# Maxima over partitions by TensorE transposes, and fewer loads for keys and values

## The chip, the cores and the metric

The kernel runs on one core of a Trainium2 chip. A core has five engines with a queue of instructions each: PE (TensorE, matmuls; the profile shows its weight loads apart, as PEld), DVE (VectorE), ACT (ScalarE), POOL (GpSimd) and SP (SyncE, which here only issues DMAs). An engine takes its queue in order, and a semaphore holds an instruction back until what it needs is there. The metric is the time of one execution on the device in microseconds, lower is better.

## The reference

Three layers follow each other, all in float32.

```python
# memory attention: B=8 batches, H=8 heads, S=576 positions, d=64, M=32 memory slots
a = exp(phi - max(phi, axis=2));  a = a / (sum(a, axis=2) + 1e-09)      # over the 576 positions
k_m = einsum('bhsm,bhsd->bhmd', a, k);  v_m = einsum('bhsm,bhsd->bhmd', a, v)
scores = q @ k_m.T / 8
attn = exp(scores - max(scores, -1));  attn = attn / (sum(attn, -1) + 1e-09)
x = (attn @ v_m) with heads side by side                                # 4608 x 512
# first feed-forward layer: w_in 512 x 2048, w_out 2048 x 512
h = x @ w_in;  x = (h - tanh(h)) @ w_out
# second: w1, w2, w3 512 x 768, w_out 768 x 512
y = maximum(maximum(x @ w1, x @ w2), x @ w3) @ w_out                    # 4608 x 512, the output
```

The softmax weights `a` need, for each batch, head and memory slot, the largest of 576 values of phi. The kernel puts positions on the 128 partitions, so this maximum runs along the free axis and then over partitions.

## The kernel before, in words

**Precision.** The two feed-forward layers and the product with attn split each operand into a high and a low float32r part and add three matmuls (`mm3`, lines 93 to 96). Weights are converted from the two halves of a 64-bit word to float32 (`conv`, lines 99 to 124: a load, ACT, five DVE instructions, POOL).

**The attention of one batch.** `load_phi` brings phi as 128 partitions x 8 heads x 5 chunks x 32 slots (the fifth chunk has 64 positions, the rest is filled with -3e38). `phi_gen` (lines 176 to 192) takes the maximum over the chunks (`mx`, DVE), then over the partitions by POOL's `partition_all_reduce` (`mxa`), subtracts it (DVE), and takes exp (ACT). `kv_mm` (lines 198 to 228) multiplies the weights with keys and values: for each parity `e` of the head, chunk `c` and head pair `r`, one float32 matmul of 32 columns of weights with 129 columns, of which 64 are keys, 64 values and one a constant one, so that the sum of the weights falls out beside. It accumulates in the PSUM tile `ps_kv`. Then come the division (`rc`, `n`, DVE), a transpose by matmuls with `ident` (`ps_t`) and the copies `kT`, `vT` (ACT). `q_gen` (lines 239 to 283) transposes the queries (DVE), makes scores (`sc`), the softmax over 32 slots, and the split weights `at`. `vw_gen` multiplies `vT` with a quarter of W_in (`wi`, from `wi_conv`) to `vw`, so that the first layer is one product of `at` and `vw`.

**Loads.** All of these DMAs are issued by SP. Keys and values of a head pair fill one of four tiles by six DMAs (`load_kv`, lines 151 to 162; 256-byte pieces in the large ones), 24 a batch. Queries are sixteen DMAs a batch in pieces of 128 bytes. phi is one tile and is loaded again for the next batch once `kv_mm` has read it, and so are the key and value tiles.

**The feed-forward stream.** A step is one 128-wide slice `fc` of the hidden layer for 288 positions: six matmuls into `ps_h` (`emit_h`), tanh on ACT, the difference on DVE (`th`), the high part on ACT and the low part on POOL (`gh`, line 404), then twelve matmuls into `ps_x` (`emit_x`). h runs three steps ahead of x, gh two. The first half of the hidden layer (phase 0) runs batch after batch beside the attention of the batches to come, the second half (phase 1) after it beside the conversion of the last layer's weights; then the last layer follows alone.

**What sets the order.** The code hands the attention's generators out in slots between the stream's matmuls, each with the step from which it may run (`kv_gen` of a batch 20 steps before its first). A prelude drains the first batch's `phi_gen`, `kv_mm`, half of `q_gen` and the first quarter of W_in (lines 480 to 486). A scheduler then rearranges the instructions of each engine by its own model of times, which moves urgent ones ahead. The PSUM pool `ps_m` has two buffers for all of `ps_kv`, `ps_t`, `sc` and `ps_w`.

Of the kernel before, what the change touches and what calls it, by code (L numbers as in the profile page):

```python
# [1 line left out]

# [4 lines left out]

F32 = mybir.dt.float32
# [3 lines left out]
ALU = mybir.AluOpType  # L12
AX = mybir.AxisListType
# [9 lines left out]
def kernel(  # L23
# [23 lines left out]
    V, S, G, T, DMA = nc.vector, nc.scalar, nc.gpsimd, nc.tensor, nc.sync  # L47
    B, H, NS, D = q.shape
    M = phi.shape[3]
    P = 128  # L50
    HP = H // 2
    C = 5
    KV = 2 * D + 2
    NKV = 4
    TJ = NS // 32
    JH = TJ // 2
    NH = NS // 2
# [9 lines left out]
    def pool(name, space=None, stack=ctx, **kw):  # L67
        if space is not None:
            kw["space"] = space
        if space is not DRAM:  # L70
            kw["reuse_waits"] = "tile"
        return stack.enter_context(tc.tile_pool(name=name, bufs=1, **kw))

    dram = pool("dram", DRAM)
    const = pool("const")
    ident = const.tile([P, P], F32, name="ident")

    main, wo_s = ExitStack(), ExitStack()
    wo_p = pool("wo", stack=wo_s, side="right")
# [5 lines left out]
    ap = pool("attn", stack=attn)  # L85
    ps_x = pool("ps_x", PSUM, main)
    ps_h = pool("ps_h", PSUM, main)
    ps_m = pool("ps_m", PSUM, main)
# [47 lines left out]
    phi_t, kv_t, q_t = {}, {}, {}  # L136

    def load_phi(b):
        if b < B and b not in phi_t:
            t = ap.tile([P, H, C, M], F32, tag="phi", bufs=1, name="phi")  # L140
            DMA.dma_start(out=t[:, :, :4], in_=phi[b, :, :4 * P].rearrange("h (p c) m -> p h c m", p=P))
            DMA.dma_start(out=t[:64, :, 4], in_=phi[b, :, 4 * P:].rearrange("h p m -> p h m"))
            G.memset(t[64:, :, 4], -3e38)
            phi_t[b] = t


    kv_s = [ap.tile([P, 2, C, KV], F32, name=f"kv{i}") for i in range(NKV)]
    kv_order = [(b, r) for b in range(B) for r in range(HP)]
    kv_next = [0]

    def load_kv():
        if kv_next[0] < len(kv_order):
            b, r = kv_order[kv_next[0]]
            t = kv_s[kv_next[0] % NKV]
            kv_next[0] += 1
            for i, x in enumerate((k, v)):
                src = x[b, 2 * r:2 * r + 2]
                o = slice(i * D, i * D + D)
                for h in range(2):
                    DMA.dma_start(out=t[:, h, :4, o], in_=src[h, :4 * P].rearrange("(p c) d -> p c d", p=P))  # L160
                DMA.dma_start(out=t[:64, :, 4, o], in_=src[:, 4 * P:].rearrange("h p d -> p h d"))
            kv_t[b, r] = t


    def load_q(b, g):
        if b < B and (b, g) not in q_t:
            t = ap.tile([P, 2, TJ, 32], F32, tag="q", bufs=2, name="qt")
            src = q[b, 4 * g:4 * g + 4].rearrange("(r e) (p j) (t d) -> e t r p j d", e=2, p=32, t=2)
            for e in range(2):
                for h in range(2):  # L170
                    for r in range(2):
                        DMA.dma_start(out=t[64 * e + 32 * h:64 * e + 32 * h + 32, r], in_=src[e, h, r])
            q_t[b, g] = t
# [3 lines left out]
    def phi_gen(b):  # L177
        load_phi(b)
        ph = phi_t.pop(b)
        yield  # L180
        mx = ap.tile([P, H, M], F32, tag="mx", bufs=1, name="mx")
        V.tensor_reduce(mx, ph.rearrange("p h c m -> p h m c"), axis=AX.X, op=ALU.max)
        yield
        mxa = ap.tile([P, H, M], F32, tag="mxa", bufs=1, name="mxa")
        G.partition_all_reduce(mxa.rearrange("p h m -> p (h m)"), mx.rearrange("p h m -> p (h m)"), P, bass_isa.ReduceOp.max)
        yield
        V.tensor_tensor(out=ph, in0=ph, in1=mxa[:, :, None, :].to_broadcast([P, H, C, M]), op=ALU.subtract)
        yield
        S.activation(ph, ph, AF.Exp)
        yield  # L190
        ph_t[b] = ph
        yield
# [5 lines left out]
    def kv_mm(b):  # L198
        ph = ph_t.pop(b)
        ps = ps_m.tile([P, 2, 256], F32, tag="m", bufs=2, name="ps_kv")  # L200
        ts = [kv_t.pop((b, r)) for r in range(HP)]
        for e in range(2):
            for c in range(C):
                pk = P if c < 4 else 64
                for r in range(HP):
                    T.matmul(ps[32 * r:32 * r + 32, e, :2 * D + 1], ph[:pk, 2 * r + e, c], ts[r][:pk, e, c, :2 * D + 1], start=c == 0, stop=c == C - 1)
                if c % 2:
                    yield
            yield
        load_phi(b + 1)  # L210
        for r in range(HP):
            load_kv()
        rc = ap.tile([P, 2], F32, tag="rc", bufs=2, name="rc")
        V.tensor_scalar(rc, ps[:, :, 2 * D], 1e-9, None, ALU.add)
        V.reciprocal(rc, rc)
        n = ap.tile([P, 2, 2, D], F32, tag="kvn", bufs=2, name="n")
        V.tensor_tensor(out=n.rearrange("p i e d -> p e i d"), in0=ps[:, :, :2 * D].rearrange("p e (i d) -> p e i d", i=2),
                        in1=rc[:, :, None, None].to_broadcast([P, 2, 2, D]), op=ALU.mult)
        yield
        pt = ps_m.tile([P, 2, P], F32, tag="m", bufs=2, name="ps_t")  # L220
        for i in range(2):
            for e in range(2):
                T.matmul(pt[64 * e:64 * e + 64, i], n[:, i, e], ident, start=True, stop=True)
        kT[b] = ap.tile([P, HP, M], F32, tag="kT", bufs=2, name="kT")
        for i, t in enumerate((kT[b], vT[b])):
            S.copy(t.rearrange("p r m -> p (r m)"), pt[:, i])
        yield

    def kv_gen(b):
        yield from phi_gen(b)  # L230
        yield from kv_mm(b)
# [134 lines left out]
    steps, start = [], {}  # L366
# [95 lines left out]

    V.memset(ident, 0.0)
    G.affine_select(ident, ident, pattern=[[-1, P]], compare_op=ALU.not_equal, fill=1.0, base=0, channel_multiplier=1)
    for t in kv_s:
        G.memset(t[:, :, :, 2 * D:], 1.0)
    def drain(*gens):
        gens = list(gens)
        while gens:
            for g in list(gens):  # L470
                try:
                    next(g)
                except StopIteration:
                    gens.remove(g)
# [3 lines left out]
            yield from g  # L478

    load_phi(0)  # L480
    for _ in range(NKV):
        load_kv()
    drain(phi_gen(0))
    drain(chain(kv_mm(0), q_gen(0, (0,))), wi_conv(0))
    drain(vw_gen(0, 0, 0))
    drain(wo_conv(0, wo_p), q_gen(0, (1,)))
# [171 lines left out]
```

## Time and profile before

| | us |
|---|---|
| median of 3 runs (1539.48 to 1541.59) | 1541.33 |
| the profiled execution | 1544.93 |
| its span | 1543.0 |
| PE busy | 1386.9 |
| DVE busy | 652.6 |
| POOL busy | 487.0 |
| ACT busy | 442.5 |

The profile shows one execution. Busy times are those of an engine at work on an instruction; waits and issues of DMAs are not counted. A row's name is "out <- in" by the program's tiles, with the line of the kernel. In the timeline and the groups, the brackets or the last column give the idle time of the engine before a row and what ended it; "issue" means that the profile shows nothing it waited for. [...]

### The profile page before, as it was taken

The page shows a single profiled execution, that of the slowest core. Times are in us where ns is not written, and L with a number is a line of the kernel's source. Part 1 is how long each engine was busy: PE and PEld are TensorE (multiplying, and loading weights), DVE is VectorE, ACT ScalarE, POOL GpSimd, SP SyncE. Part 2 cuts the span into 40 slices and gives each one's busy share as a digit, 9 for nine tenths or more (in the row PEclk, how much of TensorE's full clock was granted, in tenths as well). Part 3 has the DMA queues.
Part 4 walks back from the last instruction along what each step waited for, and adds up shares of the span by engine and source line. Part 5 has one row for each costly group of instructions (what it writes and reads, how often), then busy time and mean ns, then how long its engine had stood idle before and what let it go on. Part 6 is the DMA issues. An engine that isn't in the chain of part 4 may idle for free.

```text
span 1543.0 us, 22485 instructions
## 1 busy us (share of the span) xinstructions
PE 1386.9 (90%) x8672; PEld 1159.2 (75%) x8672; DVE 652.6 (42%) x1209; ACT 442.5 (29%) x975; POOL 487.0 (32%) x519
## 2 busy tenths in 40 slices
PE   1468596977979989999999999999999999999998
PEld 1147385866868767888799998888888888888887
DVE  3567685444454896878732322212121121221111
ACT  1224342333434444444433332111111111111110
POOL 1245452342333666656633333111111111111110
PEclk8579898988989999999999999999999999999999
DMA  7665555544441536787522117201011010100001
GB/s 172 153 135 163 145 160 126 139 120 103 105 117 47 176 101 200 252 263 239 196 97 85 48 62 255 92 14 42 21 41 48 14 42 14 48 14 21 14 14 41
DMA packets 250858, 159.81 MB, mean 104 GB/s; under 512 B 164224, under 2 KB 233856, under 8 KB 248960
## 3 DMA queue, kind: packets, MB, share of 16 engines
q1 hardware_dynamic: 249024, 145.80, 33.9%
q0 software_dynamic: 1728, 12.58, 2.2%
q8 instruction: 68, 1.11, 0.3%
q14 instruction: 38, 0.31, 0.1%
HBM read 105.64 MB, written 52.69 MB: 103 GB/s over the span
## 4 chain that ended last, share of the span: by engine, by line
PE 50%; DVE 4%; DMA 4%; POOL 1%; issue 1%; SPq 1%; ACT 1%; POOLq 0%; ACTq 0%; DVEq 0%
PE ps_w L96 10%; PE ps_w L95 10%; PE ps_w L94 10%; PE ps_o L95 3%; PE ps_o L94 3%; PE ps_o L96 3%; PE ps_x L95 3%; PE ps_x L96 3%; PE ps_x L94 2%; DMA wb_d<-cs 2%; PE ps_h L94 1%; PE ps_h L96 1%; PE ps_h L95 1%; POOL cs L123 1%; SPq L321 1%
## 5 line engine op out<-in xcount | busy, mean ns | idle before, releaser
L95 PE MATMUL ps_x<-gh,wo 128*128 128x288 f32 x1024 | 303.5, 305 | 51.0 <-POOL gh L404 50.9
L404 POOL TENSOR_TENSOR gh<-th,gh 128x288 fp32r<-128x288 f32 x256 | 220.0, 861 | 336.6 <-ACT gh L403 270.8
L96 PE MATMUL ps_x<-gh,wo 128*128 128x288 f32 x1024 | 297.9, 301 | 1.6 <-POOL wo L123 1.5
L94 PE MATMUL ps_x<-gh,wo 128*128 128x288 f32 x1024 | 263.7, 305 | 16.7 <-ACT wo L121 10.0
L96 PE MATMUL ps_w<-xh,wb 128*128 128x512 f32 x648 | 254.9, 393 | 0.0
L95 PE MATMUL ps_w<-xh,wb 128*128 128x512 f32 x648 | 254.4, 393 | 0.0
L94 PE MATMUL ps_w<-xh,wb 128*128 128x512 f32 x648 | 253.8, 392 | 0.0
L95 PEld LDWEIGHTS ps_x<-gh,wo 128*128 128x128 f32 x1024 | 197.9, 193 | 74.4 <-POOL gh L404 60.8
L598 POOL TENSOR_TENSOR mh<-m,mh 128x512 fp32r<-128x512 f32 x54 | 71.1, 1319 | 489.1 <-ACT mh L597 489.1
L401 DVE TENSOR_TENSOR th<-ps_h,th 128x288 f32<-128x288 f32 x256 | 115.5, 452 | 230.2 <-ACT th L400 230.1
L94 PEld LDWEIGHTS ps_x<-gh,wo 128*128 128x128 f32 x1024 | 181.7, 194 | 39.7 <-issue 11.9
L96 PEld LDWEIGHTS ps_x<-gh,wo 128*128 128x128 f32 x1024 | 197.6, 194 | 3.5 <-POOL wo L123 2.1
L94 PE MATMUL ps_h<-at,vw 128*128 128x288 f32 x512 | 158.7, 311 | 14.7 <-DVE th L401 13.1
L594 DVE TENSOR_TENSOR m<-ps_w,m 128x512 f32<-128x512 f32 x54 | 37.4, 692 | 305.5 <-PE ps_w L96 305.5
L403 ACT CAST gh<-th 128x288 fp32r<-128x288 f32 x256 | 110.5, 432 | 166.6 <-DVE th L401 146.3
L400 ACT ACTIVATE th<-ps_h 128x288 f32<-128x288 f32 x256 | 104.3, 409 | 186.1 <-PE ps_h L96 153.7
L95 PE MATMUL ps_h<-at,vw 128*128 128x288 f32 x512 | 153.7, 300 | 0.3 <-POOL at L279 0.3
L96 PE MATMUL ps_h<-at,vw 128*128 128x288 f32 x512 | 153.9, 301 | 0.0
L95 PEld LDWEIGHTS ps_w<-xh,wb 128*128 128x128 f32 x648 | 121.7, 188 | 27.9
L94 PEld LDWEIGHTS ps_w<-xh,wb 128*128 128x128 f32 x648 | 121.7, 188 | 27.5
L96 PEld LDWEIGHTS ps_w<-xh,wb 128*128 128x128 f32 x648 | 121.7, 188 | 27.2
L94 PEld LDWEIGHTS ps_h<-at,vw 128*128 128x128 f32 x512 | 98.7, 193 | 41.0 <-DVE th L401 23.4
(74 smaller groups left out, 1743.2 us busy)
## 6 DMA issues: line engine op xcount, KB each, us to landing
xd<-xo SPq DMA_DIRECT2D x36, 576.0 KB, 3.6
raw<-in_moe_w_out_dram SPq DMA_DIRECT2D x22, 512.0 KB, 3.5
qt<-in_q_dram SPq DMA_DIRECT2D x128, 72.0 KB, 3.1
at_d<-at SPq DMA_DIRECT2D x16, 576.0 KB, 3.6
at<-at_d SPq DMA_DIRECT2D x8, 1152.0 KB, 6.0
raw<-in_moe_w_dram SPq DMA_DIRECT2D x24, 384.0 KB, 3.6
wb_d<-cs SPq DMA_DIRECT2D x72, 128.0 KB, 2.9
xo<-xd SPq DMA_DIRECT2D x16, 576.0 KB, 4.3
```

Source lines behind the costliest of these rows:

```text
L94: T.matmul(o, w[0], x[0], start=start, stop=False)
L95: T.matmul(o, w[0], x[1], start=False, stop=False)
L96: T.matmul(o, w[1], x[0], start=False, stop=stop)
L123: G.tensor_sub(lo, f(a), f(hi))
L321: DMA.dma_start(out=wb_d[3 * g + i][:, w, kc], in_=f(t[:, :, i * P:(i + 1) * P]))
L400: S.activation(th, ps, AF.Tanh)
L401: V.tensor_sub(th, ps, th)
L403: S.copy(gh[:, 0], th)
L404: G.tensor_sub(gh[:, 1], th, f(gh[:, 0]))
L594: V.tensor_max(m, pss[1], m)
L598: G.tensor_sub(mh[:, 1], m, f(mh[:, 0]))
```

## The change

Four things are changed. The maximum over partitions goes through PE: `mx` (128 partitions x 256 columns, head and slot) is transposed in two halves into the PSUM tile `ps_mx`, DVE reduces each row to one number (`mt`, 128 x 2), multiplies it onto the diagonal of `ident` (`dg`), and a matmul of `ones` with `dg` gives every partition all 256 maxima, which the subtraction reads from PSUM. The pool's two PSUM buffers now serve `ps_mx` too. Second, keys and values of a batch lie in one tile, filled by four DMAs (1 KB pieces in the two large ones), issued once `kv_mm` of the batch before has run. Third, the sum of the weights has matmuls of its own, of one column against `ones`, ahead of the matmuls of 128 columns. Fourth, the first batch's queries are loaded before the first pieces of W_in, not after them.

```diff
-    kv_s = [ap.tile([P, 2, C, KV], F32, name=f"kv{i}") for i in range(NKV)]
...
-    def load_kv():
...
-                for h in range(2):
-                    DMA.dma_start(out=t[:, h, :4, o], in_=src[h, :4 * P].rearrange("(p c) d -> p c d", p=P))
-                DMA.dma_start(out=t[:64, :, 4, o], in_=src[:, 4 * P:].rearrange("h p d -> p h d"))
-            kv_t[b, r] = t
+    def load_kv(b):
+        if b < B:
+            t = kv_t[b] = ap.tile([P, 2, H, C, D], F32, tag="kv", bufs=1, name="kv")
+            for i, x in enumerate((k, v)):
+                DMA.dma_start(out=t[:, i, :, :4].rearrange("p h c d -> p h (c d)"), in_=x[b, :, :4 * P].rearrange("h (p c) d -> p h (c d)", p=P))
+                DMA.dma_start(out=t[:64, i, :, 4], in_=x[b, :, 4 * P:].rearrange("h p d -> p h d"))
@@ phi_gen
-        mxa = ap.tile([P, H, M], F32, tag="mxa", bufs=1, name="mxa")
-        G.partition_all_reduce(mxa.rearrange("p h m -> p (h m)"), mx.rearrange("p h m -> p (h m)"), P, bass_isa.ReduceOp.max)
-        yield
-        V.tensor_tensor(out=ph, in0=ph, in1=mxa[:, :, None, :].to_broadcast([P, H, C, M]), op=ALU.subtract)
+        pm = ps_m.tile([P, 2, 2, P], F32, tag="m", bufs=2, name="ps_mx")
+        for i in range(2):
+            T.transpose(pm[:, 0, i], mx[:, 4 * i:4 * i + 4].rearrange("p h m -> p (h m)"), ident)
+        mt = ap.tile([P, 2], F32, tag="mt", bufs=1, name="mt")
+        V.tensor_reduce(mt, pm[:, 0], axis=AX.X, op=ALU.max)
+        yield
+        dg = ap.tile([P, 2, P], F32, tag="dg", bufs=1, name="dg")
+        V.tensor_tensor(out=dg, in0=ident[:, None, :].to_broadcast([P, 2, P]), in1=mt[:, :, None].to_broadcast([P, 2, P]), op=ALU.mult)
+        T.matmul(pm[:, 1].rearrange("p i j -> p (i j)"), ones, dg.rearrange("p i j -> p (i j)"), start=True, stop=True)
+        yield
+        V.tensor_tensor(out=ph, in0=ph, in1=pm[:, 1].rearrange("p i (h m) -> p (i h) m", m=M)[:, :, None, :].to_broadcast([P, H, C, M]), op=ALU.subtract)
@@ kv_mm
-                    T.matmul(ps[32 * r:32 * r + 32, e, :2 * D + 1], ph[:pk, 2 * r + e, c], ts[r][:pk, e, c, :2 * D + 1], start=c == 0, stop=c == C - 1)
+                    T.matmul(ps[32 * r:32 * r + 32, e, 2 * D:2 * D + 1], ph[:pk, 2 * r + e, c], ones[:pk, :1], start=c == 0, stop=c == C - 1)
+            for c in range(C):
+                pk = P if c < 4 else 64
+                for r in range(HP):
+                    T.matmul(ps[32 * r:32 * r + 32, e, :2 * D], ph[:pk, 2 * r + e, c], t[:pk, :, 2 * r + e, c], start=c == 0, stop=c == C - 1)
...
-        for r in range(HP):
-            load_kv()
+        load_kv(b + 1)
...
-    for t in kv_s:
-        G.memset(t[:, :, :, 2 * D:], 1.0)
+    G.memset(ones, 1.0)
...
-    for _ in range(NKV):
-        load_kv()
+    load_kv(0)
+    load_q(0, 0)
+    load_q(0, 1)
     drain(phi_gen(0))
```

The scheduler puts the instructions of every engine in another order with it. Three places matter below. SP's queue at the start of the program, before (kv_88 to kv_91 are the four key and value tiles, raw a piece of a weight matrix, qt the queries; of the first batch's 24 loads two rows stand, and the x14 come after the 24 of the second batch, of which the last two rows stand):

```order
L141 DMA phi<-in_phi_dram 128x8x128
L142 DMA phi<-in_phi_dram 64x8x32
L160 DMA kv_88<-in_k_dram 128x4x64 x2
L161 DMA kv_88<-in_k_dram 64x2x64
...
L101 DMA raw<-in_moe_w_in_dram 128x1024 x2
L172 DMA qt<-in_q_dram 32x18x32 x2
...
L160 DMA kv_91<-in_v_dram 128x4x64 x2
L161 DMA kv_91<-in_v_dram 64x2x64
L172 DMA qt<-in_q_dram 32x18x32 x14
L101 DMA raw<-in_moe_w_in_dram 128x1024 x2
```

and now:

```order
L140 DMA phi<-in_phi_dram 128x8x128
L141 DMA phi<-in_phi_dram 64x8x32
L150 DMA kv<-in_k_dram 128x8x256
L151 DMA kv<-in_k_dram 64x8x64
L150 DMA kv<-in_v_dram 128x8x256
L151 DMA kv<-in_v_dram 64x8x64
L161 DMA qt<-in_q_dram 32x18x32 x16
L100 DMA raw<-in_moe_w_in_dram 128x1024 x2
L161 DMA qt<-in_q_dram 32x18x32 x2
...
L100 DMA raw<-in_moe_w_in_dram 128x1024
L161 DMA qt<-in_q_dram 32x18x32 x5
L100 DMA raw<-in_moe_w_in_dram 128x1024
```

The first sixteen query loads moved from behind both batches' keys and values to a place ahead of W_in; behind them, the second batch's keys and values still stand ahead of the last pieces of W_in.

[...]

```order
L404 TENSOR_TENSOR gh<-th,gh 128x288 x7
L143 MEMSET phi 64x8x32
L404 TENSOR_TENSOR gh<-th,gh 128x288
L185 ISA
L185 ISA mxa<-mx 128x256
L404 ISA
L404 TENSOR_TENSOR gh<-th,gh 128x288 x4
L273 TENSOR_TENSOR s<-s,st 128x288 x2
L404 TENSOR_TENSOR gh<-th,gh 128x288
L279 TENSOR_TENSOR at<-aT,at 128x288 x2
```

and now:

```order
L403 TENSOR_TENSOR gh<-th,gh 128x288 x8
L142 MEMSET phi 64x8x32
L403 TENSOR_TENSOR gh<-th,gh 128x288 x4
L272 TENSOR_TENSOR s<-s,st 128x288 x2
L278 TENSOR_TENSOR at<-aT,at 128x288
L403 TENSOR_TENSOR gh<-th,gh 128x288
L278 TENSOR_TENSOR at<-aT,at 128x288
```

The reduction and the ISA rows around it are gone, and gh follows gh.

PE's queue around a batch's `kv_mm` in phase 0, before (the first rows of the 40; ps_x and ps_h are the stream):

```order
L95 MATMUL ps_h<-at,vw 128x288
L96 MATMUL ps_h<-at,vw 128x288
L94 MATMUL ps_x_3052<-gh,wo_1182 128x288
L206 MATMUL ps_kv<-kv_88,phi 32x129
L206 MATMUL ps_kv<-kv_89,phi 32x129
L206 MATMUL ps_kv<-kv_90,phi 32x129
L206 MATMUL ps_kv<-kv_91,phi 32x129
L206 MATMUL ps_kv<-kv_88,phi 32x129
```

and now, in the same part of the program, with the transposes, the matmul by ones and `kv_mm` in three pieces:

```order
L175 MATMUL ps_mx<-ident,mx 128x128 x2
L93 MATMUL ps_x_2491<-gh,wo_1170 128x288
...
L95 MATMUL ps_h<-at,vw 128x288
L181 MATMUL ps_mx<-dg,ones 128x256
L93 MATMUL ps_h<-at,vw 128x288
...
L93 MATMUL ps_h<-at,vw 128x288
L202 MATMUL ps_kv<-ones,phi 32x1 x20
L206 MATMUL ps_kv<-kv,phi 32x128 x20
L202 MATMUL ps_kv<-ones,phi 32x1 x20
L206 MATMUL ps_kv<-kv,phi 32x128 x20
L93 MATMUL ps_x_2845<-gh,wo_559 128x288
```

The transposes and the matmul by ones stand between the stream's matmuls, 31 rows apart, and 44 rows ahead of `kv_mm`, which now has forty matmuls of one column beside forty of 128.

## Rows read from the trace of the kernel before

**Rows 1.** busy time by stage: length, engines (instructions), granted clock, DMA share, GB/s.

```profile
0.00:69.67 69.67, 15.91 (x121) 5.71 (x121) 26.45 (x50) 9.99 (x16) 11.66 (x21) 0.70 0.74 161
69.67:256.49 186.82, 135.01 (x1067) 106.02 (x1067) 131.61 (x248) 65.78 (x154) 83.78 (x86) 0.84 0.58 152
256.49:437.47 180.98, 152.81 (x1320) 130.54 (x1320) 83.88 (x183) 64.18 (x154) 61.39 (x79) 0.91 0.49 117
```

**Rows 2.** Waits of PE up to 560 us: total, times, longest.

```profile
PE ps_x L95 <- POOL gh L404: 50.0, 7, 10.5
...
PE ps_t L223 <- DVE n L217: 12.7, 3, 5.2
```

**Rows 3.** Timeline of POOL: start, length, instruction, [idle before <- what ended it].

```profile
371.82 1.08 POOL L185 PARTITION_ALL_REDUCE mxa<-mx  x1 [6.37 <-PE ps_h L96]
380.78 1.54 POOL L404 TENSOR_TENSOR gh<-th,gh 128x288 fp32r<-128x288 f32 x2 [7.88 <-issue]
```

**Rows 4.** Timeline of PE, same columns: first and last stall.

```profile
110.15 0.61 PE L94 MATMUL ps_x<-gh,wo 128*128 128x288 f32 x1 [9.38 <-ACT wo L121]
...
437.47 0.61 PE L95 MATMUL ps_x<-gh,wo 128*128 128x288 f32 x1 [9.00 <-POOL gh L404]
```

**Rows 5.** Busy time by stretch, as rows 1: after the stalls, and their sum.

```profile
110.15:119.50 9.35, 9.35 (x43) 6.96 (x44) 5.10 (x15) 3.90 (x9) 3.62 (x6) 0.50 0.17 26
192.26:198.00 5.74, 5.74 (x34) 4.55 (x35) 2.92 (x8) 2.39 (x7) 1.10 (x2) 0.50 0.37 95
...
sum 35.08, PE 35.07 PEld 27.61 DVE 17.72 ACT 11.52 POOL 13.22; mean PE 5.85 PEld 4.60 DVE 2.95 ACT 1.92 POOL 2.20
```

**Rows 6.** Timeline of PE and of its weight loads (PEld): kv_mm, ps_t.

```profile
293.98 0.30 PE L95 MATMUL ps_x<-gh,wo 128*128 128x288 f32 x1
294.12 0.29 PE L96 MATMUL ps_x<-gh,wo 128*128 128x288 f32 x1
294.34 2.82 PE L206 MATMUL ps_kv<-kv,phi 128*32 128x129 f32 x80
...
294.34 0.82 PEld L206 LDWEIGHTS ps_kv<-kv,phi 128*32 128x32 f32 x32 [0.16 <-issue]
295.36 0.15 PEld L206 LDWEIGHTS ps_kv<-kv,phi 64*32 64x32 f32 x8 [0.20 <-issue]
...
364.41 0.66 PE L223 MATMUL ps_t<-ident,n 128*64 128x128 f32 x8
```

**Rows 7.** The tile ps_kv: duration in ns, least/median/most.

```profile
L206 PE MATMUL ps_kv<-kv,phi x640: 270/273/424, 12.0 to 481.4; 128*32 128x129 f32 x128, 64*32 64x129 f32 x32
```

**Rows 8.** Groups by line, to 800 us: busy us, mean ns, idle before.

```profile
L182 DVE TENSOR_REDUCE mx<-phi 128x256 f32<-128x1280 f32 x8 | 19.4, 2424 | 12.5 <-DMA phi<-in_phi_dram 12.5
...
L187 DVE TENSOR_TENSOR phi<-phi,mxa 128x1280 f32<-128x1280 f32 x8 | 11.9, 1492 | 32.1 <-POOL mxa L185 32.1
...
L189 ACT ACTIVATE phi<-phi 128x1280 f32<-128x1280 f32 x8 | 10.2, 1269 | 42.9 <-DVE phi L187 37.4 <-DMA kv<-in_v_dram 5.5
...
L217 DVE TENSOR_TENSOR n<-ps_kv,rc 128x256 f32<-128x256 f32 x8 | 3.3, 418 | 0.1
```

**Rows 9.** Timeline of SP's queue (SPq), the first 70 us.

```profile
2.04 1.30 SPq L160 DMA_DIRECT2D kv<-in_k_dram  x2
...
17.35 0.63 SPq L161 DMA_DIRECT2D kv<-in_v_dram  x1
...
40.27 9.38 SPq L172 DMA_DIRECT2D qt<-in_q_dram  x14
49.77 1.41 SPq L101 DMA_DIRECT2D raw<-in_moe_w_in_dram  x2
```

**Rows 10.** Timeline of PE, the first 72 us.

```profile
19.08 4.95 PE L206 MATMUL ps_kv<-kv,phi 128*32 128x129 f32 x74 [3.53 <-DMA kv<-in_v_dram]
...
47.58 1.30 PE L257 MATMUL sc<-qT,kT 64*32 64x288 f32 x8 [17.33 <-DVE qT L248]
...
69.67 0.61 PE L94 MATMUL ps_h<-at,vw 128*128 128x288 f32 x1 [0.67 <-ACT vw L298]
```

More of the change, by code (lines that the diff above doesn't have):

```diff
@@ L4 @@
 import concourse.tile as tile
-from concourse import bass_isa, mybir
+from concourse import mybir
 from concourse._compat import with_exitstack
@@ L52 @@
     C = 5
-    KV = 2 * D + 2
-    NKV = 4
     TJ = NS // 32
@@ L76 @@
     ident = const.tile([P, P], F32, name="ident")
+    ones = const.tile([P, P], F32, name="ones")
     main, wo_s = ExitStack(), ExitStack()
@@ L144, in load_phi @@
             phi_t[b] = t
-    kv_s = [ap.tile([P, 2, C, KV], F32, name=f"kv{i}") for i in range(NKV)]
-    kv_order = [(b, r) for b in range(B) for r in range(HP)]
-    kv_next = [0]
-    def load_kv():
[L152 to L155, printed above, removed]
-            for i, x in enumerate((k, v)):
-                src = x[b, 2 * r:2 * r + 2]
-                o = slice(i * D, i * D + D)
-                for h in range(2):
-                    DMA.dma_start(out=t[:, h, :4, o], in_=src[h, :4 * P].rearrange("(p c) d -> p c d", p=P))
-                DMA.dma_start(out=t[:64, :, 4, o], in_=src[:, 4 * P:].rearrange("h p d -> p h d"))
-            kv_t[b, r] = t
+    def load_kv(b):
+        if b < B:
+            t = kv_t[b] = ap.tile([P, 2, H, C, D], F32, tag="kv", bufs=1, name="kv")
+            for i, x in enumerate((k, v)):
+                DMA.dma_start(out=t[:, i, :, :4].rearrange("p h c d -> p h (c d)"), in_=x[b, :, :4 * P].rearrange("h (p c) d -> p h (c d)", p=P))
+                DMA.dma_start(out=t[:64, i, :, 4], in_=x[b, :, 4 * P:].rearrange("h p d -> p h d"))
     def load_q(b, g):
@@ L200, in kv_mm @@
         ps = ps_m.tile([P, 2, 256], F32, tag="m", bufs=2, name="ps_kv")
-        ts = [kv_t.pop((b, r)) for r in range(HP)]
+        t = kv_t.pop(b)
         for e in range(2):
```

## The prediction

> **What bounds the kernel now.** I read the stage table first, then who TensorE waits for, then the timeline of the engine that it names. The stage table [rows 1] cuts the span at the first matmul that makes h (69.67 us), after the fourth batch's reduction on POOL (256.49) and after the last (437.47). Behind that no instruction is added or taken away. Up to 69.67 us PE is busy for 15.91 of 69.67 us: a prelude of loads and preparation. From there to 437.47 us PE is busy for 135.01 of 186.82 and 152.81 of 180.98 us, at a mean granted clock of 0.84 and 0.91. DVE is the next engine: 131.61 of 186.82 us in the middle, 83.88 of 180.98 after it.
>
> The waits [rows 2] put the largest share of PE's idle time on POOL's gh: 50.0 us in seven waits. The timeline of POOL around one of them [rows 3] shows why. The reduction over partitions is a row of 1.08 us, but POOL stands idle 6.37 us ahead of it and 7.88 us behind it, with nothing that it waits for: from 365.45 (371.82 less 6.37) to 380.78 us POOL makes no gh, and PE, two steps ahead at most, runs dry. It happens once a batch; the first two batches fall into the prelude, and six stalls are left, the first and the last of which stand in [rows 4]: 9.38 + 10.48 + 10.03 + 9.35 + 9.82 + 9.00 = 58.06 us. (The first is put down to ACT's wo cast, which itself waited for POOL.) [...]
>
> [...]
>
> **The change, part by part.**
>
> *POOL's reduction goes.* In the new order of POOL gh follows gh at that place, with no custom instruction, so no stretch of [rows 3] is left: -58.1 us and -17.5 us, if nothing else is late at those places.
>
> *PE gets new work, which goes straight onto the path.* The column of ones leaves the value tile, so kv_mm issues 40 more matmuls of one column a batch, 80 in the profile's records, which show each of these float32 matmuls twice. The old 80 take 2.82 us at full clock [rows 6], with weights loaded every 0.82/32 = 26 ns, and 0.20 us lost where the shape changes from 128 to 64 rows or back. One column can hardly go faster than its weight load: 80 x 26 ns = 2.05 us, and four more changes of shape are 0.8 us, 2.85 in all. Bounds: 1 us, if such a matmul hides in its neighbours; 5.4 us, if the twenty records of a column group follow each other at the 0.27 us that one of the old ones lasts [rows 7]. I take 2.85, since the weight loads are the same. The two transposes and the matmul by ones are six records; eight of the ps_t row take 0.66 us [rows 6], so 0.5 us and about 0.35 us to fill twice: 0.85. That is 3.7 us a batch, 1.5 to 6.2. Batch 0's share is in the prelude; seven are 25.9 us.
>
> *DVE gets two small instructions*, the maximum over 256 PSUM elements and the diagonal: each like the 0.418 us of n, a 256-element read of PSUM [rows 8]. The subtraction stays 1.49 us. 0.84 us a batch, beside PE in the last stage, and counted below in the middle one.
>
> *A chain PE - DVE - PE - DVE - ACT takes the place of POOL's.* PE now waits in its queue for the maxima (transposes) and for the diagonal (matmul by ones), and behind the waiting matmul stand the next h and x matmuls. In the new order some 30 matmul rows lie between the two, about 4 us of PE work at 0.13 to 0.14 us each, the distance of two in [rows 6], and 44 more, 5.9 us, from there to kv_mm. The chain needs 0.6 + 0.42 + 0.42 us up to the first and about 0.45 + 1.49 + 1.27 us [rows 8] and the hops up to the second. That fits where DVE has slack, as it does after 256 us (46% busy [rows 1]): nothing. Where DVE is behind, the nearest row is PE's wait for n, 5.2 us at longest and 12.7 us in three waits over eight batches [rows 2]; I keep 0 to 5 us for each of batches 1 to 3, and put it into the price of the middle stage.
>
> *Loads.* Keys and values were 24 issues a batch at 0.64 us, the first batch from 2.04 to 17.98 us [rows 9], and their last bytes started kv_mm at 19.08 [rows 10]. Now they are four issues, done by about 5 us. The sixteen query loads follow at 9.38/14 = 0.67 us (up to 15.6), then the first two pieces of W_in at 16.5, as before. Before, queries were issued from 40.27 to 49.65 us, so the scores waited 17.33 us and began at 47.58; now all queries can be there at 20. The second pair of W_in was issued at 49.77 us, since the next batch's keys and queries stood ahead of it in SP's queue, and 18.5 us after that issue ended the first h matmul ran (51.18 to 69.67). In the new queue two queries, phi and the four loads of the next batch, then five queries stand ahead of the last piece of W_in: 13 issues, 8.7 us, from the end of kv_mm at 20 to 24 us. It also needs the buffer of the second piece, whose conversion stands on DVE behind the next batch's maximum, which waits for phi (about 29 us) and takes 2.42 us [rows 8]: 33 to 34 us. With the same 18.5 us behind it the first h matmul comes at about 52.5: 17 us earlier. Bounds: 8, if DVE's waits for loads add up so that the last piece goes out at 43; 25, if it goes out at 26. Batch 0's maxima go through PE and two more DVE instructions, about 1 us later than now, under loads that land later still: nothing.
>
> **The sum**, against the profiled execution's 1544.93 us (span 1543.0 and 1.9 around it). Prelude: -17. Middle (69.67 to 256.49): three stalls -29.9, clock -7.5 (half of 9.35 + 5.74), PE work of batches 1 to 4 +14.8; that leaves 164 us for 134 us of DVE work, 82% on an engine that takes its queue in order and waits for ACT in between. I add 8 us for that and for the new chain (0 to 20): -14.6. Last three batches: -28.2, clock -10.0, PE +11.1: -27.1. After that the stages do the same work; the scheduler sets some conversions of weights in another order there, which I price at nothing (5 us either way). Together -58.7, so 1486.2. The median shown is 1541.33, 3.6 below the profiled execution: 1483.
>
> **Rivals.**
> - *DVE takes the bound in the middle.* For it: 131.61 us busy there [rows 1] and PE's waits for n [rows 2]. Against it: its sum still leaves 30 us. If the middle gives back nothing beyond its added work and the prelude gives 8: -8 - 27 = -35, 1506.
> - *The added PE work hides.* If one-column matmuls cost 1 us a batch, DVE keeps up, and the prelude gives 25: -25 - 75.6 + 7 x 1.9 + 4 = -83, 1458.
> - *PE's queue pays for the chain: slower.* Every batch PE stands at the matmul by ones until DVE, which is behind, has made the diagonal. The price is that wait times seven; from (75.6 + 17 - 25.9)/7 = 9.5 us a batch on the change loses, and at 12 us the time is 1559. For it: PE waits in order with all h and x matmuls behind. Against it: the longest such wait for DVE is 5.2 us, and only three stand in eight batches [rows 2]. [...]
> [...]
>
> **How the numbers follow.** Forecast (1470 to 1497) 0.61, DVE-bound middle (1497 and up) 0.18, of which 0.01 within 0.2%, hidden PE work (under 1470) 0.17, POOL not freed 0.02, PE's queue pays 0.02. Eight in ten: 1460 to 1512, which takes in most of the DVE-bound case and of the bounds on the one-column matmuls. About 0.2% (3 us) is what a measurement of this kernel can tell from no change: faster 0.95, within 0.01, slower 0.04.
>
> **What would show it.** In the changed profile: no POOL idle stretch of 6 to 8 us put down to issue, and no PE wait of 9 us for gh; granted clock 1.0 from about 240 us on; ps_kv 160 records in about 5.7 us a batch; the first h matmul near 52 us; PE's waits for ps_mx under 1 us in the last batches, up to 5 in the first. Wrong would be: waits at ps_mx of 5 us and more in every batch, a first h matmul after 62 us, or DVE over 90% busy between the first h matmul and the fourth batch.

## The result and the profile after

The changed kernel takes 1484.35 us in the median (four runs, 1481.26 to 1487.11) against 1541.46 before: a ratio of 0.963, 95% interval 0.9608 to 0.9653. The forecast was 1483. The profiled execution took 1483.24 us with a span of 1481.5, 61.6 us less than the 1543.05 of before (forecast: 58.7 less).

The stage table of the changed kernel, cut where PE has done as many matmuls of x as at the cuts of [rows 1] (the first h matmul, x matmul 411, x matmul 987, each to within one matmul; columns as there, the granted clock as a share of full speed):

```profile
0.00:59.82 59.82, 19.13 (x205) 7.55 (x205) 26.29 (x49) 7.83 (x14) 9.60 (x16) 1.00 0.86 197
59.82:223.53 163.71, 142.91 (x1301) 112.17 (x1302) 135.04 (x254) 67.46 (x153) 81.23 (x83) 0.87 0.57 161
223.53:376.41 152.88, 150.51 (x1577) 131.80 (x1576) 84.62 (x190) 64.07 (x155) 57.70 (x76) 0.99 0.51 129
```

The prelude is 9.85 us shorter, the middle 23.1 and the last three batches 28.1; what is behind them, 0.5. In the last three batches PE is now idle for 2.4 of 152.88 us. The clock of 1.00 in the first row is no measurement: the clock's records begin at 74.7 us, and up to there matmuls of 288 columns follow each other at 0.24 us, as they do at a granted clock of 0.50 (88.77 to 89.97 us), not at the 0.13 us that they take behind it, at 1.00:

```profile
73.82 0.45 PE L94 MATMUL ps_h<-at,vw 128*128 128x288 f32 x1
74.06 0.45 PE L95 MATMUL ps_h<-at,vw 128*128 128x288 f32 x1
...
75.96 0.30 PE L93 MATMUL ps_x<-gh,wo 128*128 128x288 f32 x1
76.09 0.30 PE L94 MATMUL ps_x<-gh,wo 128*128 128x288 f32 x1
```

Who PE waits for up to 560 us (total, times, longest), where [rows 2] stood before:

```profile
PE ps_w L294 <- POOL wi L116: 13.3, 2, 10.3
PE ps_h L93 <- DVE th L400: 11.6, 9, 2.8
PE ps_h L93 <- ACT at L277: 10.8, 3, 9.3
PE ps_t L222 <- DVE n L216: 10.3, 1, 10.3
PE ps_mx L175 <- DVE mx L171: 7.7, 1, 7.7
...
PE ps_x L94 <- POOL gh L403: 1.3, 5, 0.6
PE ps_mx L181 <- DVE dg L180: 1.0, 1, 1.0
```

The 50.0 us for gh are 1.3. The waits for `wi`, n and mx stand in the prelude. In place of POOL's stretch of [rows 3], the timeline of POOL around a batch's maxima (transposes at 312.95, matmul by ones at 317.15):

```profile
311.88 0.80 POOL L403 TENSOR_TENSOR gh<-th,gh 128x288 fp32r<-128x288 f32 x1 [2.81 <-ACT gh L402]
314.25 0.91 POOL L403 TENSOR_TENSOR gh<-th,gh 128x288 fp32r<-128x288 f32 x1 [1.58 <-ACT gh L402]
316.97 0.80 POOL L403 TENSOR_TENSOR gh<-th,gh 128x288 fp32r<-128x288 f32 x1 [1.80 <-PE ps_x L95]
```

POOL waits for ACT's part of gh, or for a matmul of x, and nothing here is put down to issue; the longest such stretch up to 560 us is 4.7 us.

For all runs the span can be taken apart by PE's records: each counts until the next one starts, half of the time at a granted clock of 0.50 is set apart (up to the first clock record too; the half is an estimate from these 0.24 and 0.13 us), and the rest is idle. The last 5 us, after PE's last matmul, are left out. The rows for h, x, scores, `ps_t` and the last layer move by up to 4.3 us each and are summed in "other".

| us | before | after | e1 | e2 | e3 | e4 | e5 | e6 | e7 |
|---|---|---|---|---|---|---|---|---|---|
| PE idle | 151.3 | 75.5 | 87.6 | 149.2 | 68.8 | 101.6 | 70.8 | 75.7 | 64.3 |
| lost to the lower clock | 37.5 | 36.6 | 25.6 | 46.9 | 25.5 | 50.0 | 30.0 | 33.6 | 31.7 |
| `ps_kv`, keys and values | 23.3 | 21.3 | 22.7 | 22.7 | 21.6 | 21.5 | 21.6 | 21.5 | 21.6 |
| `ps_kv`, ones | 0 | 7.9 | 0 | 8.7 | 8.1 | 7.9 | 8.3 | 8.1 | 8.2 |
| `ps_mx` | 0 | 4.4 | 4.6 | 0 | 4.4 | 4.5 | 4.5 | 4.4 | 4.3 |
| `ps_w`, vw and last layer | 519.6 | 524.8 | 527.9 | 514.8 | 528.9 | 503.9 | 523.6 | 510.2 | 514.6 |
| other | 806.1 | 805.8 | 807.1 | 811.0 | 807.8 | 806.0 | 807.9 | 806.1 | 801.0 |

From before to after: idle -75.8, clock -0.9, keys and values -2.0, ones +7.9, maxima +4.4, `ps_w` +5.2. The last layer's part of `ps_w` is 448.0 to 448.1 us in all of them but e7, where it is 444.6, so that row's other differences are the vw product's.

### The profile page after: what moved, and what is told of

It reads as the page before. It is cut to its first block, busy times and chain, and to the rows that moved or that the text cites. A ratio compares the mean times of both kernels' runs of the same rounds, so it can differ in the third digit from the quotient of the medians.

```text
span 1481.5 us, 23564 instructions
## 1 busy us (share of the span) xinstructions
PE 1401.1 (95%) x9344; PEld 1167.8 (79%) x9344; DVE 657.2 (44%) x1225; ACT 443.9 (30%) x975; POOL 475.3 (32%) x508
## 4 chain that ended last, share of the span: by engine, by line
PE 77%; DVE 10%; DMA 5%; SPq 4%; issue 2%; ACT 2%; POOL 1%; DVEq 0%; POOLq 0%; ACTq 0%
PE ps_w L95 10%; PE ps_w L94 10%; PE ps_w L93 10%; PE ps_x L93 7%; PE ps_x L94 7%; PE ps_x L95 7%; PE ps_h L93 4%; PE ps_h L94 3%; PE ps_h L95 3%; PE ps_o L94 3%; PE ps_o L93 3%; PE ps_o L95 3%; PE ps_w L294 3%; SPq L161 2%; DVE cvb L110 2%
## 5 line engine op out<-in xcount | busy, mean ns | idle before, releaser
L94 PEld LDWEIGHTS ps_x<-gh,wo 128*128 128x128 f32 x1024 | 195.2, 191 | 26.5 <-issue 16.0
L93 PEld LDWEIGHTS ps_x<-gh,wo 128*128 128x128 f32 x1024 | 180.1, 192 | 24.7 <-issue 14.2
L95 PEld LDWEIGHTS ps_x<-gh,wo 128*128 128x128 f32 x1024 | 194.8, 191 | 0.7 <-issue 0.5
L93 PE MATMUL ps_h<-at,vw 128*128 128x288 f32 x512 | 160.0, 313 | 27.6 <-DVE th L400 15.8
```

The source lines that it names most:

```text
L93: T.matmul(o, w[0], x[0], start=start, stop=False)
L94: T.matmul(o, w[0], x[1], start=False, stop=False)
L95: T.matmul(o, w[1], x[0], start=False, stop=stop)
```

## The experiments

**e1: the maxima alone.** The kernel before with the new `phi_gen` (and `ones`), its own loads, its own order of queries and its column of ones.

```diff
-        mxa = ap.tile([P, H, M], F32, tag="mxa", bufs=1, name="mxa")
-        G.partition_all_reduce(mxa.rearrange("p h m -> p (h m)"), mx.rearrange("p h m -> p (h m)"), P, bass_isa.ReduceOp.max)
...
+        pm = ps_m.tile([P, 2, 2, P], F32, tag="m", bufs=2, name="ps_mx")
...
```

> Only the maxima go through TensorE; loads, queries and the column of ones stay as before. Theory (the gain after the prelude is POOL's freedom alone): no gh stall of 9 us, first h matmul at 69 to 71 us as before, no one-column matmuls (7 x 1.07 = 7.5 us less than in the changed kernel), three more runs of the vw product than there (3 us): 1484 + 9.9 - 7.5 + 3 = 1490 us (1480 to 1500). Rival (the 24 loads a batch also hold kv_mm back once POOL no longer does): PE waits for kv of some us in every batch, 1505 us or more.

Measured: 1484.65 us, ratio 0.9629 (0.9608 to 0.9651), no different from the full change. First h matmul at 69.13 us, and no wait for gh among the larger ones:

```profile
PE sc L265 <- DVE qT L256: 20.5, 2, 15.8
PE ps_h L95 <- DVE th L409: 14.5, 14, 3.0
PE ps_mx L187 <- DVE mx L183: 7.9, 1, 7.9
```

The maxima carry the whole gain. The other three parts together bring nothing on top: the table shows 12.1 us less idle with them and 11.0 more lost to the clock, 7.9 for ones less 1.4 for keys and values, and 3.1 less in vw.

**e2: all but the maxima.** The changed kernel with POOL's reduction put back.

```diff
-        pm = ps_m.tile([P, 2, 2, P], F32, tag="m", bufs=2, name="ps_mx")
...
+        mxa = ap.tile([P, H, M], F32, tag="mxa", bufs=1, name="mxa")
+        G.partition_all_reduce(mxa.rearrange("p h m -> p (h m)"), mx.rearrange("p h m -> p (h m)"), P, bass_isa.ReduceOp.max)
...
```

> The changed kernel with POOL's reduction put back; four loads a batch, ones matmuls and queries ahead of W_in stay. Theory (loads are worth the prelude and no more): the six gh stalls of 9 to 10 us are back, first h matmul near 60 us; against the kernel before -9.9 for the prelude, +7.5 for seven batches of ones matmuls, -5 for five runs of vw fewer: 1534 us (1525 to 1545). Rival (the loads carry a good part of the gain): 1515 us or less.

Measured: 1561.78 us, ratio 1.0129 (1.0111 to 1.0147): 20 us slower than before, worse than either theory. The first h matmul is at 62.86 us, 6.8 earlier. But the first 96 matmuls of x take until 146.30 us, against 131.57 before, and PE's waits up to 560 us are

```profile
PE ps_x L94 <- POOL gh L396: 65.6, 6, 12.3
PE ps_w L287 <- POOL wi L116: 17.0, 3, 11.1
PE ps_kv L195 <- ACT phi L178: 13.8, 1, 13.8
PE ps_h L93 <- ACT at L270: 10.0, 2, 8.6
```

The six stalls are 7.5 us longer together than the 58.1 of before, one wait of 8.6 us for the second batch's at is new, the clock costs 9.4 us more and the ones 8.7; the prelude has 8.5 us less idle time. The longer stalls begin at POOL: ahead of the six reductions it is idle for 7.5 to 9.7 us, where it was 6.0 to 6.4 before. Why it is longer in this order stays open.

**e3: the queries behind W_in again.** The changed kernel without its fourth part.

```diff
-    load_q(0, 0)
-    load_q(0, 1)
     drain(phi_gen(0))
```

> The changed kernel without the fourth part: the first queries are no longer issued ahead of W_in. Theory (W_in's conversion is what the first h waits for, and 16 query loads of 1 us each stand ahead of it): W_in's first pieces issued near 9 us instead of 24.7, all four by 35 instead of 47, first h matmul at 45 to 52 us instead of 59.8; five more runs of vw (+5): 1477 us (1468 to 1484). Rival (the scores set the first h, so queries first is right): scores later by about 10 us, first h at 60 us or later, 1489 us or more.

Measured: 1471.22 us, ratio 0.9541 (0.9527 to 0.9555): 13 us faster than the full change. SP's queue (SPq) of the changed kernel, and then of e3:

```profile
4.80 4.03 SPq L151 DMA_DIRECT2D kv<-in_v_dram  x1
8.87 15.82 SPq L161 DMA_DIRECT2D qt<-in_q_dram  x16
24.73 1.09 SPq L100 DMA_DIRECT2D raw<-in_moe_w_in_dram  x2
...
37.66 1.53 SPq L100 DMA_DIRECT2D raw<-in_moe_w_in_dram  x1
...
46.72 0.56 SPq L100 DMA_DIRECT2D raw<-in_moe_w_in_dram  x1
```

```profile
9.04 2.05 SPq L100 DMA_DIRECT2D raw<-in_moe_w_in_dram  x2
11.13 17.64 SPq L161 DMA_DIRECT2D qt<-in_q_dram  x16
28.91 1.01 SPq L100 DMA_DIRECT2D raw<-in_moe_w_in_dram  x2
```

The first h matmul then stands at 49.75 us in place of 59.82 (timelines of PE, e3 first):

```profile
49.75 0.85 PE L93 MATMUL ps_h<-at,vw 128*128 128x288 f32 x2 [1.49 <-ACT at L277]
```

```profile
52.24 1.92 PE L294 MATMUL ps_w<-wi,vT 64*32 64x512 f32 x4 [10.26 <-POOL wi L116]
57.23 1.92 PE L294 MATMUL ps_w<-wi,vT 64*32 64x512 f32 x4 [3.08 <-POOL wi L116]
59.82 0.61 PE L93 MATMUL ps_h<-at,vw 128*128 128x288 f32 x1 [0.67 <-ACT vw L297]
```

The prelude waits for W_in's conversion, and the queries stood in its way. Part four alone costs the change 13 us. So parts two and three, all that separates e3 from e1, gain 13 us beside the new maxima (1471.22 against 1484.65), and part four takes them back.

**e4: vw's matmuls ahead of the stream's.**

```diff
-        for r in range(HP):
-            for e in range(2):
+        with tc.high_priority():
+          for r in range(HP):
+            for e in range(2):
```

> The changed kernel with the scheduler told to issue the matmuls of the vw product ahead of the stream's as soon as they can run. In order they then stand in 52 runs instead of 74, with the same 256 matmuls. Theory (a run costs about 0.97 us whether it has one matmul or eight, since those of different 32-column and 64-row parts run side by side): 22 runs less, 21 us less, 1463 us (1455 to 1472). Rival (the single rows only look long, the cost is per matmul): 1484 us as now. Second rival (vw ahead of the stream makes h and x late): 1490 us or more with new waits of PE.

Measured: 1490.15 us, ratio 0.9652 (0.963 to 0.9674; its four runs spread from 1484.04 to 1502.62, and the profiled one is the slowest). The price of a run holds: `ps_w` falls by 20.9 us where 21 were expected. So does the second rival: idle time rises by 26.1 us and the loss to the clock by 13.4. Both are the slowest run's; by the medians e4 is 5.8 us behind the changed kernel, and the ranges of the two overlap. PE's waits from 60 to 880 us name the places:

```profile
PE ps_h L93 <- DVE th L401: 21.5, 14, 7.3
PE ps_h L93 <- ACT at L277: 9.7, 2, 8.8
PE ps_w L295 <- DVE s L261: 9.2, 4, 3.1
PE ps_x L93 <- DVE xo L440: 3.9, 3, 1.6
```

In the changed kernel the wait for th is 15.8 there and the one for s 2.0. Fewer runs are worth their price only where nothing else is made late.

**e5: the second batch's maxima in the prelude.** On top of e3.

```diff
-    drain(chain(kv_mm(0), q_gen(0, (0,))), wi_conv(0))
+    drain(chain(kv_mm(0), q_gen(0, (0,)), phi_gen(1)), wi_conv(0))
...
-    fg.add("kv", kv_gen(1))
+    fg.add("kv", kv_mm(1))
```

> As e3_q_last, and the second batch's maxima, subtraction and exp are issued in the prelude, behind the first scores, not after the first h matmuls (the transposes stood at 55.6 us there though their input was ready some 20 us earlier). Theory (the 8.2 us wait of PE for the second batch's at, at 107 us, hangs on this chain, held up in PE's queue): transposes at 36 to 42 us, the wait gone, 1455 to 1465 us against 1471. Rival (DVE, 88% busy between the first h and 120 us, sets it and the chain only waits elsewhere): the wait of at stays or moves, 1466 to 1474 us (four runs of vw fewer are 4 us of that).

Measured: 1474.01 us, ratio 0.9551 (0.9528 to 0.9575), no gain over e3. The transposes moved from 55.62 to 38.55 us and the second batch's `kv_mm` from 71.6 to 53.0, yet the wait for at is still there:

```profile
105.00 0.85 PE L93 MATMUL ps_h<-at,vw 128*128 128x288 f32 x2 [8.12 <-ACT at L277]
```

The theory falls: the chain through `ps_mx` does not set that wait. It ends 9 to 10 us behind the last scores, in e3 (98.28 to 107.14) as in e5 (95.06 to 105.00).

**e6: e4's edit in the second half of the hidden layer alone,** on top of e3.

```diff
+        with tc.high_priority() if ph else nullcontext():
```

> As e3_q_last, with the vw product's matmuls ahead of the stream's in the second half of the hidden layer alone, where no attention uses the same PSUM buffers: 59 runs instead of 79. Theory (e4_vw_first lost by vw's waits for PSUM buffers held by scores, which the second half has not): 20 runs by 0.9 us less, 1453 us (1447 to 1460). Rival (vw ahead of the stream makes th and gh late whatever the half): new PE waits behind DVE's th, 1467 us or more.

Measured: 1464.78 us, ratio 0.95 (0.9483 to 0.9516), the fastest of the kernels here that leave nothing out. `ps_w` falls by 18.7 us, as by the theory, but the time by 6.4 only: 6.9 us come back as idle time, 8.1 as loss to the clock. Some of that stands ahead of the edit, whose new order reaches back: at x matmul 1537, the first of the second half, e6 is 2.7 us behind e3, at the last 5.3 ahead. So the second half gives 8.0 of the 18.7 us. The time lies between the two ranges, and both theories hold in part: from 440 to 870 us the waits for th, which the rival expected to grow, are 9.2 us against 9.0 in e3, but the waits ahead of x matmuls are 11.3 us against 3.3.

**e7: less work for DVE.** The changed kernel with a shorter conversion.

```diff
-        V.tensor_scalar(a, b, 0xFF800000, None, ALU.bitwise_and)
-        V.scalar_tensor_tensor(out=f(a), in0=lw, scalar=2.0 ** -52, in1=f(a), op0=ALU.mult, op1=ALU.mult)
...
-        G.tensor_add(f(a), f(b), f(a))
+        G.tensor_add(f(a), f(b), zero.to_broadcast([P, n]))
```

> The changed kernel, but every weight conversion leaves out the low word: two of its five DVE instructions (0.42 + 0.68 us of 2.65 us) are gone, POOL adds a zero column instead; the weights are a little less exact. Theory (between the first h matmul and 130 us DVE is 93% busy and PE waits for it, and the gaps keep the clock at 0.50): DVE share there under 80%, the 9.3 us wait for at mostly gone, half the loss to the clock gone, seven runs of vw fewer, 1445 to 1468 us against 1484. Rival (the length of the attention's chain sets these waits, not DVE's sum): only vw's 7 us, 1474 to 1482 us.

Measured: 1455.42 us, ratio 0.9441 (0.9426 to 0.9457): 29 us less than the changed kernel, as the theory had it, but not where. From the first h matmul to the 97th of x, the changed kernel and then e7 (columns as in the stage table):

```profile
59.82:130.20 70.38, 55.18 (x423) 37.19 (x423) 65.12 (x122) 27.82 (x59) 35.26 (x34) 0.78 0.63 172
```

```profile
52.22:122.17 69.95, 53.81 (x436) 36.76 (x437) 55.77 (x108) 28.32 (x63) 34.15 (x37) 0.84 0.76 201
```

DVE's share falls from 93% to 80%, and the stretch gets hardly shorter; the wait for at is 8.4 us against 9.3, and the clock costs 2.3 us less there, 4.9 in all. PE is idle for 16.1 us of the stretch against 15.2, so it is not shown that the gaps keep the clock at 0.50. Of the 30.5 us between the two profiled executions 7.6 are in the prelude (first h at 52.22), 0.4 in this stretch, 6.6 from there to x matmul 987, and 15.9 behind it, where vw stands in 42 runs instead of 53 and takes 10.8 us less. So DVE's sum does not set the wait for at either.

What is left is the order of DVE's queue. The changed kernel's rows ahead of that at (W_in's conversion writes cva, the softmax st, and qT belongs to queries to come):

```profile
112.57 0.39 DVE L268 TENSOR_REDUCE st<-s 128x9 f32<-128x288 f32 x1
112.88 1.05 DVE L112 TENSOR_SCALAR cva<-cvb 128x512 uint32<-128x512 uint32 x1
113.85 1.42 DVE L247 STREAM_TRANSPOSE qT<-qt 128x576 f32<-128x576 f32 x2
115.21 0.12 DVE L269 TENSOR_SCALAR st<-st 128x9 f32<-128x9 f32 x1
```

From the last scores to the cast of at, 8 of DVE's 22 instructions are W_in's conversion (5.0 us); in e7 they are 5 (2.6 us), in e1, where PE's wait is 3.5 us, none. That points at the order, but no run changes it alone, so it is not shown as the cause.

## Why the prediction was right

The time was right, and so was its main step. Four other terms were off and cancelled: the clock (outside the prelude) and the prelude brought some 22 us less than forecast, PE's added work and DVE cost some 25 us less. That the sum came out so close is luck.

- **POOL's stalls: right.** -58.1 us of stalls and no new ones: 50.0 us of waits for gh became 1.3, and e1 shows that this edit alone makes the gain. The idle time ahead of the reduction is put down to PE in [rows 3], not to nothing; but it is 5.9 to 6.4 us ahead of all eight reductions, whatever ended it, so the forecast's reading stands. What POOL does in that time no row shows.
- **PE's added work: mis-sized, and below its lower bound.** Forecast 3.7 us a batch (1.5 to 6.2), measured (7.9 - 2.0 + 4.4) / 8 = 1.3. The term that failed is "one column can hardly go faster than its weight load" at 26 ns. The 26 ns were a pace that goes with matmuls of 129 columns, not the least that the weight load needs. At full clock (granted 1.00 from 323.34 to 325.31 us) a batch now shows, PE and then its weight loads:

```profile
323.34 0.60 PE L202 MATMUL ps_kv<-ones,phi 128*32 128x1 f32 x40
323.88 1.43 PE L206 MATMUL ps_kv<-kv,phi 128*32 128x128 f32 x40
```

```profile
323.34 0.52 PEld L202 LDWEIGHTS ps_kv<-ones,phi 128*32 128x32 f32 x40 [0.16 <-issue]
323.87 0.81 PEld L206 LDWEIGHTS ps_kv<-kv,phi 128*32 128x32 f32 x32
```

  The same loads of 32 columns take 0.52/40 = 13 ns ahead of one column and 0.81/32 = 25 ns ahead of 128. From the start of the first row to the next matmul of the stream it is 3.8 us a batch (forecast: about 5.7), against 2.82 for the old 80 of [rows 6]. No run shows the 0.35 us a batch to fill that the forecast added for the maxima: `ps_mx` took 4.4/8 = 0.55 us a batch in all, for 0.85.
- **The clock: wrong.** The forecast's 17.5 us are half of the 35.08 us that PE worked at a granted clock of 0.50 behind the six stalls [rows 5]. No run shows that such stretches take half as long at 1.00; what the runs show is that matmuls of 288 columns follow each other at 0.24 us at 0.50 and at 0.13 at 1.00. The 17.5 us were counted as a gain; the whole loss went from 37.5 to 36.6 us. By stage, before and after: prelude 7.9 and 9.6, middle 16.1 and 21.9, last three batches 6.9 and 1.7, behind them 6.6 and 3.4. After 250 us the clock came back as forecast (3.1 us of it behind the last cut, where the sixth stretch of [rows 5] lies), but for two spells of 3.4 us at 521.9 and 603.8. In the middle the smaller waits took the stalls' place: around the 9.26 us of idle time that end at 116.83 the granted clock falls to 0.50 at 108.9 and stays there to 132.7:

```profile
81.50:91.80 10.30, 10.03 (x176) 8.05 (x175) 9.27 (x14) 4.31 (x9) 7.55 (x8) 0.50 0.58 186
108.90:132.70 23.80, 15.76 (x54) 6.37 (x54) 22.99 (x51) 8.61 (x19) 13.59 (x13) 0.50 0.71 184
146.40:153.20 6.80, 5.84 (x25) 5.44 (x24) 5.98 (x12) 3.19 (x9) 3.24 (x4) 0.50 0.49 162
```

  The step that failed is that the middle's loss goes with its stalls: its idle time fell from 51.8 to 20.8 us, and its loss rose. The length of that one wait does not set it either: e3, with 8.2 us there, loses 14.6 us in the middle, e1, with 3.5 us, loses 17.1. What sets it stays open.
- **The chain through DVE: right.** PE waits at `ps_mx` in the prelude alone, 7.7 us for the first batch's `mx` and 1.0 us for its `dg`; behind it no wait for either is in the list. The 7.7 us are more than the 5 allowed for the first batches, but the row that they end at is PE's first, at 7.68 us, where it has no other work yet.
- **DVE in the middle: right in its share, wrong in its price.** The forecast share of 82% came out as 135.04/163.71 = 82%. Its 8 us did not come as idle time: the middle's idle time fell by 31.0 us, more than its three stalls of 29.9. What the middle lost instead is in the clock, 5.8 us more where 7.5 less were forecast; e7, with less work for DVE, gets back 2.5 of it, so most of it is not shown to be DVE's. Together the middle gave 23.1 us for 14.6, since added work was 2.2 there and not 14.8.
- **The prelude: inside its bounds, but the step on the queue failed.** -9.85 for -17. The queries were priced at 0.67 us an issue, from [rows 9], and took 15.82/16 = 0.99, with the DMA engines busy for 0.86 of the prelude against 0.74 before. They also began at 8.87 us and not at about 5, since the fourth load of keys and values alone took 4.03 us to issue. W_in's first pieces went out at 24.73 us, not at 16.5 (18.03 before), and the last at 46.72, not at 33 to 34; what stands behind the last took 13.1 us and not 18.5. e3 shows what the forecast did not ask: whether queries ahead of W_in are a gain at all.
- **The later stages: right, -0.5 us,** as a sum of -5.9 idle, -3.1 clock and +8.5 work. Most of that work is vw's, split into 74 runs by the new order where there were 67.
- **The rivals.** POOL was freed, PE's queue did not pay, and the DVE-bound middle did not come. "The added PE work hides" was nearest to what happened to that term, though not to the time.

e2 shows what a sum of parts hides: three parts that together come to nothing beside the new maxima (e1 against the full change) cost 20 us beside the old ones. The forecast priced each part alone and had no term for such a coupling.

## What to carry to other kernels

Where idle time of POOL on both sides of an instruction goes away with it, as here (6.37 and 7.88 us around the reduction), it belongs to the instruction's price, and the wait for POOL's next output is where it shows: price a replacement by that stretch, not by the row's 1.08 us. Do not book the clock's recovery with a stall that is removed (here the middle's loss to the clock rose by 5.8 us); look at which waits stay in that stage. And ahead of moving a load forward, look at which load the first matmul waits for now: here it was W_in, and the queries that were moved ahead of it cost 13 us.

## What the runs showed of the hardware

A run of vw's matmuls takes about 1 us with one matmul or with seven (records show each of these float32 matmuls twice; changed kernel, PE):

```profile
705.99 1.04 PE L294 MATMUL ps_w<-wi,vT 64*32 64x512 f32 x2
...
707.69 1.08 PE L294 MATMUL ps_w<-wi,vT 64*32 64x512 f32 x14
```

The seven use different parts of 64 rows and 32 columns of the array (`64*32` in the rows, `vw_gen` in the kernel). Up to the start of PE's next row it is 1.01 us for them and 0.97 for the one: the seven run side by side, and a lone one costs as much as all of them. The vw product stands in 67 runs before, 74 after and 52 in e4, and e4's 22 fewer took 20.9 us from PE's work. The records of matmuls of one column follow each other at 13 ns (40 records, 20 matmuls, in 0.52 us). And an issue of the same query load takes 0.67 us in one place of SP's queue, 0.99 in another and 17.64/16 = 1.10 in e3, where the DMA engines are busy for 0.90 of the prelude.
